# A two-layer network behind attention: the second layer's products, buffers and addresses rearranged

## The chip, the core and the metric

The kernel runs on one core of a Trainium2 chip. That core has a matrix engine (PE; its weight loads are shown apart as PEld), a vector engine (DVE), a scalar engine (ACT), a third elementwise engine (POOL) and a queue engine (SP) that issues most of the transfers; sixteen DMA engines carry those. Matrix products land in PSUM, eight banks of 512 fp32 columns; everything else lies in SBUF, 128 partitions wide. The metric is the device time of one execution in microseconds (us); less is better. A comparison of this kernel can tell about 0.3% from no change.

## The reference

Eight batches of eight heads, 576 tokens, head width 64: causal attention with a decay that is cumulated along the sequence, then a two-layer network with a leaky ReLU whose slope `alpha` differs for each hidden unit.

```python
scores = scale * np.matmul(q, k.transpose(0, 1, 3, 2))
cum = np.cumsum(np.log(np.clip(f, 0.0001, 1.0)), axis=-1)
decay = cum[:, :, :, None] - cum[:, :, None, :]
scores = np.where(causal, -1e9, scores + decay)
attn = softmax(scores)            # row maximum taken off first
x = np.matmul(attn, v)            # -> 4608 tokens x 512
h = x @ w_in                      # 512 -> 2048 hidden units
g = np.maximum(h, 0.0) + alpha * np.minimum(h, 0.0)
out = g @ w_out                   # 2048 -> 512
```

## The kernel before

**Precision.** Most products are made of fp32 numbers cut into a high and a low part in the format fp32r. A product of two such numbers takes three matmuls: high by high, high by low, low by high.

**Attention and the first layer.** For each of 32 pairs of heads the scores, the exponentials and the values are computed; `quotient` writes a normalised x slot. Six x slots of two parts lie in the tile `xx`. `ffn1(b)` takes one batch's 512 tokens through the first layer: 16 blocks `fc` of hidden units, for each 12 matmuls of 512 columns into one bank, then ACT (L1032 or L1035) and for most batches DVE (L1037) move the bank into one of three `hs` slots, and SP writes the slot to the DRAM tensor `hd` (L1039), 2 KB for each partition. The ninth "batch" is the last 64 tokens of each of the eight, gathered in `xt`. The matmuls of `ffn1` are spread between those of the attention from 70 us on, and stand alone from about 545 to 642 us.

**The second layer, `ffn2(u)`.** 18 units `u` of 256 tokens follow each other in the order of `UNITS`. Each is a product of 256 tokens x 2048 by 2048 x 512, cut once into quarters in Winograd's form of Strassen's scheme, so that seven products of 128 tokens by 256 columns stand in place of eight. The 16 blocks of hidden units are paired to eight `c`, taken two at a time: four groups `g`. For each group

- SP loads 512 KB from `hd` into an `hr` slot (L1252), in pieces of 1 KB,
- for the batches in `LATE`, which are 6 of the 18 units, ACT (L1262) and DVE (L1267) finish the leaky ReLU,
- DVE makes the sums S1 to S4 in a `gx` slot (L1272 to L1275, four instructions of 256 columns),
- ACT makes the high parts of the seven operands (L1288, three instructions) in a `gh` slot, and DVE the low parts (L1291, three instructions of 256, 512 and 1024 columns),
- PE runs 2 x 7 products of three matmuls of 256 columns each (L364, from L1306): 42 matmuls.

The weights lie in `wot`, seven combinations for each `c`, with all high parts ahead of all low parts. There are three `gh` slots; the third begins its life when `xx` is free of x. A unit holds four of the eight banks from its first matmul until its end, when ACT copies one half bank (L1314) and DVE adds the banks up in four instructions (L1318, L1319, L1322, L1323) into the single `hs` result, which SP writes out (L1354). The last unit has an end of its own (L1325 to L1345).

**What sets the order.** The class `Plan` holds all operations with estimated times, dependencies and keys, and plays them against each other; the order in which it picks them is the order in which each engine's instructions are issued. Buffers (`Buf`, `Ring`, `Store`) are handed out in that play, banks too. An engine issues its instructions strictly in that order and waits at each for its inputs.

**Addresses.** Five tables of 64 bytes stand ahead of `wi`, so that `wi` and every large tile behind it begin 64 bytes past a multiple of 128.

Of the kernel before, what the change touches and what calls it, by code (L numbers as in the profile page):

```python
# [9 lines left out]
F32 = mybir.dt.float32  # L10
# [195 lines left out]
def attention_moe(  # L206
# [23 lines left out]
    hd = dram.tile([NW, 2, 128, NT], F32, name="hd")  # L230
# [8 lines left out]
    am = const.tile([128, NF], F32, name="am")  # L239
    psum = ctx.enter_context(tc.tile_pool(name="psum", bufs=1, space=PSUM))  # L240
# [4 lines left out]
    xx = xp.tile([128, 6 * 2 * 512], F32R, name="xx")  # L245
# [41 lines left out]
    xs = xp.tile([128, 2 * S], F32, name="xs")  # L287
    rxs = Ring(Store([xs[:, S * i : S * i + S] for i in range(2)]))
    rri = ring(xp, 1, [128, 4, 6, 32], F32, "ri")
# [6 lines left out]
    tri = sp.tile([128, 128], BF16, name="tri")  # L296
    tri2 = sp.tile([128, 64], BF16, name="tri2")
# [717 lines left out]
    def ffn1(b):  # L1015

        for fc in range(NF):
# [16 lines left out]
            else:  # L1034
# [5 lines left out]
                hd[fc % NW, fc // NW, :, 512 * b : 512 * b + 512], bs.t), -1000, [cp], [bs], kb=256)  # L1040
# [79 lines left out]
    rhr = ring_later(2, [128, GW, 2, TU], F32, "hr")  # L1120
    rgx = ring_later(1, [128, 4, GW, 128], F32, "gx")
# [6 lines left out]
    wot = [None] * (NW - NV) + [wid[:, WN * i : WN * i + WN].rearrange("p (k j n) -> p k j n", k=2, j=7) for i in range(NV)]  # L1128

    def change():  # L1130
# [8 lines left out]
        for i in range(NW - NV):  # L1139
            wot[i] = p1.tile([128, 2, 7, 256], F32R, name=f"wot{i}")  # L1140
        rP.least = 0

    def change3():
        st = rhr.store
        for i in range(4):
            st.free.append((plan.t, len(st.items)))
            st.items.append(wx[0].rearrange("p a (b c j) n -> p (a b) c j n", b=2, c=GW)[:, i])

    def change2():
        n = 2 * 7 * GW * 128  # L1150
# [10 lines left out]
    def change5():  # L1161
        rgx.store.free.append((plan.t, len(rgx.store.items)))
        rgx.store.items.append(xs[:, 0:1024].rearrange("p (i c q) -> p i c q", i=4, c=GW))

    o_change = op("-", 0, change, 0, done_a)
    for c in (0, 2):
        bt_ = Buf(rhr)
        tv = lambda bt_=bt_: bt_.t.rearrange("p c j t -> p c (j t)")
        ld = op("SP", 400, lambda c=c, tv=tv: sy.dma_start(tv(), xt[c : c + 2].rearrange("c p t -> p c t")), 1e6, [o_change] + xt_ops, [bt_], kb=512)
        for i in range(2):  # L1170
            bx = Buf(rx)
            xh = op("ACT", c_acs(512), lambda i=i, bx=bx, tv=tv: ac.activation(bx.t[:, 0], tv()[:, i], AF.Copy), 1e4, [ld], [bt_, bx])
            xl = op("DVE", c_dve(512), lambda i=i, bx=bx, tv=tv: ve.tensor_tensor(
                bx.t[:, 1], tv()[:, i], bx.t[:, 0].bitcast(F32), ALU.subtract), 1e4, [xh], [bt_, bx], two=True)
            x_ops[B, c + i] = (bx, xh, xl)
# [9 lines left out]
    def load_w_out(c):  # L1185
# [214 lines left out]
```

## Time and profile before

| | us |
|---|---|
| median of the runs (lowest to highest) | 1012.02 (1010.92 to 1013.88) |
| profiled execution, its own time | 1010.48 |
| profiled execution, span from first to last instruction | 1008.7 |
| busy in the span: PE, PEld | 999.0, 888.5 |
| busy in the span: DVE, ACT, POOL | 803.7, 606.8, 394.6 |

The span falls into three stretches. Up to about 545 us the attention and the first layer are mixed; until 642 us the first layer stands alone; from 642 us to the end there is only the second layer. In that last stretch POOL has nothing to do. The clock granted to PE was full in all of them. Busy times of PE count a matmul until its modelled end, so that overlapping matmuls make a busy engine; rates are better read from the starts or from counts in a stretch.

### The profile page before, as it was taken

The page shows a single profiled execution, that of the slowest core. Times are in us where ns is not written, and L with a number is a line of the kernel's source. Part 1 is how long each engine was busy: PE and PEld are TensorE (multiplying, and loading weights), DVE is VectorE, ACT ScalarE, POOL GpSimd, SP SyncE. Part 2 cuts the span into 40 slices and gives each one's busy share as a digit, 9 for nine tenths or more (in the row PEclk, how much of TensorE's full clock was granted, in tenths as well). Part 3 has the DMA queues.
Part 4 walks back from the last instruction along what each step waited for, and adds up shares of the span by engine and source line. Part 5 has one row for each costly group of instructions (what it writes and reads, how often), then busy time and mean ns, then how long its engine had stood idle before and what let it go on. Part 6 is the DMA issues. An engine that isn't in the chain of part 4 may idle for free.

```text
span 1008.7 us, 22200 instructions
## 1 busy us (share of the span) xinstructions
PE 999.0 (99%) x7900; PEld 888.5 (88%) x7900; DVE 803.7 (80%) x1745; ACT 606.8 (60%) x1369; POOL 394.6 (39%) x635
## 2 busy tenths in 40 slices
PE   9999999999999999999999999999999999999998
PEld 6778888888888788888888888999999999999998
DVE  7878768888877848868655987788898888989994
ACT  7987876666666645656444766564554645546551
POOL 4575758799988858869740100000000000000000
PEclk9999999999999999999999999999999999999999
DMA  7988748889887887968766666633534344434411
GB/s 225 264 241 245 227 130 230 238 250 264 257 242 211 260 242 206 260 206 233 235 174 241 212 205 212 207 116 123 157 113 142 115 140 132 139 115 137 135 55 42
DMA packets 130686, 191.12 MB, mean 189 GB/s; under 512 B 22088, under 2 KB 79728, under 8 KB 130576
## 3 DMA queue, kind: packets, MB, share of 16 engines
q1 hardware_dynamic: 124400, 170.66, 55.7%
q0 software_dynamic: 5888, 18.85, 7.4%
q8 instruction: 62, 1.02, 0.4%
q14 instruction: 48, 0.39, 0.1%
q10 hardware_dynamic: 288, 0.20, 0.1%
HBM read 102.74 MB, written 48.80 MB: 150 GB/s over the span
## 4 chain that ended last, share of the span: by engine, by line
PE 93%; DMA 3%; DVE 2%; ACT 1%; SPq 1%; POOL 1%; issue 0%; DVEq 0%; ACTq 0%
PE bank L364 89%; PE bank L584 2%; DMA big<-big 1%; SPq L920 1%; DVE big L883 1%; DMA rd<-st 0%; DMA vr<-in_vv_dram 0%; PE bank L432 0%; DMA rqk<-in_qk_dram 0%; ACT big L826 0%; DVE Z L491 0%; PE bank L466 0%; POOL Z L510 0%; ACT big L580 0%; POOL Qhl L538 0%
## 5 line engine op out<-in xcount | busy, mean ns | idle before, releaser
L364 PE MATMUL bank<-xx,wi 128*128 128x512 f32 x1728 | 407.7, 392 | 1.8 <-DVE st L846 1.8
L364 PEld LDWEIGHTS bank<-xx,wi 128*128 128x128 f32 x1728 | 319.8, 188 | 68.4 <-DVE st L846 2.2
L826 ACT ACTIVATE big<-big,st 128x384 f32<-128x384 f32 (+4 forms) x207 | 118.6, 575 | 44.3 <-DVE st L846 44.3
L1037 DVE SCALAR_TENSOR_TENSOR hs<-bank,sa,hs 128x512 f32<-128x512 f32 x96 | 71.2, 743 | 79.0 <-ACT hs L1035 78.8
L364 PE MATMUL bank<-wi,gh 128*128 128x256 f32 x1008 | 123.9, 283 | 0.0
L364 PE MATMUL bank<-wot,gh 128*128 128x256 f32 x1008 | 123.9, 283 | 0.0
L364 PEld LDWEIGHTS bank<-wot,gh 128*128 128x128 f32 x1008 | 122.3, 192 | 0.1
L364 PEld LDWEIGHTS bank<-wi,gh 128*128 128x128 f32 x1008 | 122.3, 192 | 0.0
L1035 ACT ACTIVATE hs<-bank,ab 128x512 f32<-128x512 f32 x96 | 66.1, 689 | 88.3 <-PE bank L364 70.5
L883 DVE STREAM_TRANSPOSE big<-big 128x1408 f32<-128x1408 f32 (+2 forms) x69 | 86.6, 1273 | 22.3 <-DMA hd<-hs 6.7
L364 PEld LDWEIGHTS bank<-big,vr 128*64 128x64 f32 x1884 | 88.9, 137 | 12.0 <-issue 3.9
L364 PE MATMUL bank<-big,vr 128*64 128x128 f32 (+2 forms) x1884 | 95.5, 259 | 2.0 <-DVE st L609 1.1
L538 POOL TENSOR_TENSOR Qhl<-rqk,Qhl 128x640 fp32r<-128x640 f32 (+1 forms) x56 | 83.3, 1496 | 30.8 <-ACT Qhl L537 29.1
L920 POOL DMA_DIRECT2D big<-big x184 | 92.1, 507 | 7.9 <-DVE big L883 4.2
L364 PE MATMUL bank<-Qhl 64*128 64x512 f32 (+6 forms) x840 | 93.1, 326 | 0.1
L364 PEld LDWEIGHTS bank<-Qhl 64*128 64x128 f32 (+1 forms) x840 | 74.9, 186 | 15.8 <-issue 9.1
L510 POOL TENSOR_TENSOR Z<-Z,tri 128x384 f32<-128x384 f32 x60 | 54.6, 922 | 27.9 <-DMA Z<-c 18.5
L364 PE MATMUL bank<-wot,xx 128*128 128x256 f32 x504 | 62.4, 283 | 0.0
L364 PE MATMUL bank<-wi,xx 128*128 128x256 f32 x504 | 62.4, 283 | 0.0
L364 PEld LDWEIGHTS bank<-wi,xx 128*128 128x128 f32 x504 | 61.3, 192 | 0.0
L364 PEld LDWEIGHTS bank<-wot,xx 128*128 128x128 f32 x504 | 61.3, 192 | 0.0
L1032 ACT ACTIVATE hs<-bank,sg 128x512 f32<-128x512 f32 x48 | 33.0, 687 | 33.3 <-PE bank L364 28.4
(176 smaller groups left out, 1501.5 us busy)
## 6 DMA issues: line engine op xcount, KB each, us to landing
hd<-hs SPq DMA_DIRECT2D x144, 256.0 KB, 3.6
wx<-hd SPq DMA_DIRECT2D x46, 512.0 KB, 3.8
big<-big SPq DMA_DIRECT2D x184, 100.0 KB, 5.1
big<-big POOLq DMA_DIRECT2D x184, 100.0 KB, 4.9
rqk<-in_qk_dram SPq DMA_DIRECT2D x28, 608.0 KB, 5.1
hr<-hd SPq DMA_DIRECT2D x26, 512.0 KB, 3.5
vr<-in_vv_dram SPq DMA_DIRECT2D x32, 320.0 KB, 4.4
big<-in_w_in_dram SPq DMA_DIRECT2D x16, 512.0 KB, 6.1
```

The source lines that it names most:

```text
L364: pe.matmul(o, lhsT, rhs, start=start, stop=stop)
L510: m1 = op("POOL", c_po(128 * 3), lambda z4=z4: po.tensor_tensor(z4()[:, 6:9], z4()[:, 0:3], tb(3), ALU.add), kc + 0.1, got + [o_mask], [bZ])
L538: o2 = op("POOL", c_po(w), lambda hi=hi, lo=lo, raw=raw: po.tensor_tensor(lo(), raw(), hi().bitcast(F32), ALU.subtract), kc, [o1], [bqk, bQ])
L584: pe.transpose(t[:, c : c + 128], src[:, 128 * j : 128 * j + 128], ident)
L826: sums.append(op("ACT", c_exp(w), lambda: ac.activation(at(), at(), AF.Exp, bias=lo()[:, col : col + 1], scale=-1.0, accum_out=su()[:, col ...
L883: ve.transpose(t_t[:, :, c0 : c0 + 32 * (b1 - b0)].rearrange("p k (b c) -> p k b c", c=32), bE.t[:, 128 * off : 128 * (off + b1 - b0)].rea ...
L920: moves.append(op(n_, 550 if i % 2 else 450, lambda a=a, k=k, q_=q_: q_.dma_start(bM.t[32 * k : 32 * k + 32, a], t_t[32 * a : 32 * a + 32, ...
L1032: cp = op("ACT", c_act(512), lambda bh=bh, bs=bs, fc=fc: ac.activation(bs.t, bh.t, AF.Copy, scale=sg[:, fc : fc + 1]), -1000, [last, o_sg] ...
L1035: cp = op("ACT", c_act(512), lambda bh=bh, bs=bs, fc=fc: ac.activation(bs.t, bh.t, AF.Relu, scale=ab[:, fc : fc + 1]), -1000, [last, o_sg] ...
L1037: cp = op("DVE", c_dve(512), lambda bh=bh, bs=bs, fc=fc: ve.scalar_tensor_tensor(bs.t, bh.t, sa[:, fc : fc + 1], bs.t, ALU.mult, ALU.add), ...
```

## The change

The second layer is rewritten, and tiles change places.

- **Products.** In all units but the last, three of the seven products (numbers 0, 2 and 5) put the high operand against the high and the low weights in one matmul of 512 columns, and then the low operand against the high weights in one of 256. `wot` is laid out so that a combination's high and low parts are neighbours. Such a product fills a whole bank, whose halves are added at the end; a unit holds five banks, taken one after the other as they are first used, and its products run one after the other for both `c` of a group. `rO` may hold all eight banks.
- **The unit's end.** DVE adds one half bank (L1357), the two halves of two banks (L1327, four instructions of 256 columns), then as before (L1330, L1333, L1334): eight instructions in place of four.
- **A group.** Raw and summed operands share a slot of `hg` (8 KB, five slots in the end, in place of six `hr` and two `gx`). The sums take three instructions (512, 256, 256 columns), the high parts two, the low parts one of 1792 columns. The third `gh` slot and one `hg` slot are laid over the old x slots by a pool of their own (`change2`).
- **`hd`** is laid out by batch and group, so that a group's load is two runs of 2 KB for each partition; the first layer's write becomes four runs of 512 bytes.
- **Addresses.** `xx` goes to the upper end of SBUF; `hs`, `xs`, `ri`, `tri` and `tri2` become parts of one tile `hx`; 64 bytes are left free behind the five tables. `wi`, `hx`, `xx`, `big`, `gh`, `hg`, `wx` and `wot` all begin at a multiple of 128 bytes.

The diff, cut to what matters:

```diff
-    hd = dram.tile([NW, 2, 128, NT], F32, name="hd")
+    hd = dram.tile([B + 1, NW // GW, 128, 2, 2, 2, GW, 128], F32, name="hd")
...
+    const.tile([128, NF], F32, name="rest_c")
...
-    xx = xp.tile([128, 6 * 2 * 512], F32R, name="xx")
+    ctx_x = ExitStack()
+    xq = ctx_x.enter_context(tc.tile_pool(name="xq", bufs=1, side="right"))
+    xx = xq.tile([128, 6 * 2 * 512], F32R, name="xx")
+    xq.tile([128, 24], F32, name="rest_x")
...
-    rH, rO = Ring(banks, 2, 4), Ring(banks, 0, 6)
+    rH, rO = Ring(banks, 2, 4), Ring(banks, 0, 8)
...
-    hs = xp.tile([128, 7 * 256], F32, name="hs")
+    hx = xp.tile([128, 3840], F32, name="hx")
+    hs = hx[:, 2048:3840]
...
             hd_ops[b, fc] = op("SP", 400, lambda bs=bs, fc=fc: sy.dma_start(
-                hd[fc % NW, fc // NW, :, 512 * b : 512 * b + 512], bs.t), -1000, [cp], [bs], kb=256)
+                hd[b, fc % NW // GW, :, fc // NW, :, :, fc % GW].rearrange("p u i q -> p (u i) q"), bs.t.rearrange("p (k q) -> p k q", q=128)), -1000, [cp], [bs], kb=256)
...
-            wot[i] = p1.tile([128, 2, 7, 256], F32R, name=f"wot{i}")
+            wot[i] = p1.tile([128, 7, 2, 256], F32R, name=f"wot{i}")
...
-    PRODS = ((0, 0, 3, 0), (1, 1, 2, 0), (2, 6, 0, 1), (3, 3, 1, 0), (4, 5, 1, 1), (5, 4, 2, 1), (6, 2, 0, 0))
+    PRODS = ((0, 0, 3, 0), (2, 1, 2, 0), (1, 6, 0, 1), (4, 3, 1, 0), (3, 5, 1, 1), (5, 4, 2, 1), (6, 2, 0, 0))
...
+        twice = (0, 2, 5) if wide else ()
+        parts = [[PRODS[i] for i in k] for k in ((0,), (1, 5), (3, 4), (2, 6))] if wide else (PRODS[:3], PRODS[3:])
...
-            o2 = op("DVE", 4 * c_dve(128 * GW), sums, key, [o1], [bhr, bgx], two=True)
...
+            h0 = op("ACT", c_acs(3 * 128 * GW), lambda bhx=bhx, bgh=bgh: ac.activation(bgh.t[:, 0, 0:3], bhx.t[:, 1:4], AF.Copy), key, o1, [bhx, bgh])
+            o2 = op("DVE", c_tt(256 * GW) + 2 * c_tt(128 * GW), sums, key, o1, [bhx], two=True)
+            h1 = op("ACT", c_acs(4 * 128 * GW), lambda bhx=bhx, bgh=bgh: ac.activation(bgh.t[:, 0, 3:7], bhx.t[:, 4:8], AF.Copy), key, [o2], [bhx, bgh])
...
+                        if ia in twice:
+                            bank = 4 if ia == 5 else bank
+                            mm(bo[bank].t, bgh.t[:, 0, ia, cc], wot[c][:, ib].rearrange("p k n -> p (k n)"), c == 0, False)
+                            mm(bo[bank].t[:, 0:256], bgh.t[:, 1, ia, cc], wot[c][:, ib, 0], False, c == NW - 1)
+                            continue
...
-        e1 = op("DVE", 2 * c_dve(512), ends, -500, [e0], bo[:3] + [bs])
-        e2 = op("DVE", c_dve(512) + c_dve(256), ends2, -500, [e1], bo[:2] + [bs])
+        e1 = op("DVE", c_tt(256), lambda: ve.tensor_tensor(bs.t[:, 3], bo[3].t[:, :256], bs.t[:, 3], ALU.add), -500, [e0], [bo[3], bs])
+        for i, k in ((0, 2), (4, 4)):
+            e1 = op("DVE", 2 * c_tt(256), lambda i=i, k=k: both(i, k), -500, [e1, ends_of[-5]], [bo[k], bs])
+        e1 = op("DVE", c_tt(512), ends, -500, [e1, ends_of[-3]], [bo[1], bs])
+        e2 = op("DVE", c_tt(512) + c_tt(256), ends2, -500, [e1, last], [bo[0], bo[1], bs])
```

Two places of the order. On PE, one `c` of a group in the second layer before (number 0 in the first unit; `x3` and `x6` count equal matmuls that follow each other, each with its weight load):

```order
L364 MATMUL bank6_82<-wot0_6096,gh0_6093 128x256 x3
L364 MATMUL bank1_77<-wot0_6096,gh0_6093 128x256 x3
L364 MATMUL bank5_81<-wot0_6096,gh0_6093 128x256 x3
L364 MATMUL bank3_79<-wot0_6096,gh0_6093 128x256 x6
```

(the second and the third row follow once more behind these) and after, the first group of the second unit, whose two `c` are `wot0` and `wot1`:

```order
L372 MATMUL bank0_77<-wot0_6095,gh1_6093 128x512
L372 MATMUL bank0_77<-wot0_6095,gh1_6093 128x256
L372 MATMUL bank0_77<-wot1_6096,gh1_6093 128x512
L372 MATMUL bank0_77<-wot1_6096,gh1_6093 128x256
L372 MATMUL bank7_84<-wot0_6095,gh1_6093 128x512
L372 MATMUL bank7_84<-wot0_6095,gh1_6093 128x256
L372 MATMUL bank4_81<-wot0_6095,gh1_6093 128x512
L372 MATMUL bank4_81<-wot0_6095,gh1_6093 128x256
```

Three matmuls of 256 columns became one of 512 and one of 256; behind these rows come the same four for `wot1` and then 24 matmuls of 256 columns into two more banks.

On DVE, the end of a unit among the next groups' work before (L1318 to L1323 are the end):

```order
L1291 TENSOR_TENSOR gh1_6094<-xs_107,gh1_6094 128x1024
L1318 TENSOR_TENSOR hs_92<-bank4_80,hs_92 128x2x256
L1319 TENSOR_TENSOR hs_92<-bank0_76,hs_92 128x512
L1322 TENSOR_TENSOR hs_92<-bank2_78,hs_92 128x512
L1323 TENSOR_TENSOR hs_92<-bank0_76,hs_92 128x256
L1291 TENSOR_TENSOR xx_88<-hr0_6090,xx_88 128x256
```

and after (L1357 to L1334 are the end, with a group's low parts, L1294, in the middle of it):

```order
L1357 TENSOR_TENSOR hx_97<-bank7_84,hx_97 128x256
L1327 TENSOR_TENSOR hx_97<-bank3_80,hx_97 128x256 x2
L1327 TENSOR_TENSOR hx_97<-bank4_81,hx_97 128x256 x2
L1330 TENSOR_TENSOR hx_97<-bank5_82,hx_97 128x512
L1294 TENSOR_TENSOR gh2_6866<-wx_6094,gh2_6866 128x1792
L1333 TENSOR_TENSOR hx_97<-bank1_78,hx_97 128x512
L1334 TENSOR_TENSOR hx_97<-bank5_82,hx_97 128x256
L1294 TENSOR_TENSOR gh0_6092<-wx_6094,gh0_6092 128x1792
```

The end has eight instructions in place of four, and it begins while the unit's last group still runs. Until the last batches of the first layer the order of every engine is the same as before.

## Rows read from the trace of the kernel before

**Rows 1.** Page, part 1: busy us, share of the span, instructions.

```profile
PE 999.0 (99%) x7900; PEld 888.5 (88%) x7900; DVE 803.7 (80%) x1745; ACT 606.8 (60%) x1369; POOL 394.6 (39%) x635
```

**Rows 2.** Stretches: length, busy us (instructions) by engine, granted clock, DMA share, GB/s.

```profile
230.00:340.00 110.00, 107.75 (x916) 89.97 (x914) 86.34 (x212) 68.17 (x183) 95.34 (x156) 1.00 0.85 246
700.00:750.00 50.00, 50.00 (x419) 50.00 (x418) 44.01 (x80) 26.56 (x48) 0.00 (x0) 1.00 0.42 131
```

**Rows 3.** The chain that ended last: 283 to 341 us by line; its piece behind that.

```profile
by line: DMA big<-big 22.0%; SPq L920 13.5%; DVE big L883 10.2%; DMA rd<-st 7.7%; DMA rqk<-in_qk_dram 7.2%; ACT big L826 6.0%; issue 3.9%; DVE Z L491 3.9%; POOL Z L510 3.0%; POOL Qhl L538 2.5%; PE bank L364 2.3%; DVE Zt L493 2.3%; POOL xx L
...
340.57 664.55 PE bank L364 x5064
```

**Rows 4.** A stretch of 10 us in the first layer alone, PE only.

```profile
560.00:570.00 10.00, 10.00 (x46) 1.00 0.83 262
```

**Rows 5.** PE in the second layer, in order of time: start, us, line, tiles, shape, count.

```profile
702.55 10.24 PE L364 MATMUL bank<-wot,gh 128*128 128x256 f32 x84
712.63 5.20 PE L364 MATMUL bank<-wi,xx 128*128 128x256 f32 x42
```

**Rows 6.** Groups by line and shape: busy us, mean ns, idle before.

```profile
L364 PE MATMUL bank<-xx,wi 128*128 128x512 f32 x1728 | 407.7, 392 | 1.8 <-DVE st L846 1.8
L1291 DVE TENSOR_TENSOR gh<-gx,gh 128x1024 fp32r<-128x1024 f32 x24 | 29.3, 1219 | 2.0 <-ACT gh L1288 2.0
L1291 DVE TENSOR_TENSOR gh<-wx,gh 128x256 fp32r<-128x256 f32 x34 | 14.2, 418 | 0.0
L1267 DVE TENSOR_TENSOR wx<-wx,gx 128x1024 f32<-128x1024 f32 x7 | 8.5, 1220 | 0.0
```

**Rows 7.** DVE in order of time: a unit's end, a group's low parts, sums.

```profile
702.45 0.69 DVE L1318 TENSOR_TENSOR hs<-bank,hs 128x512 f32<-128x512 f32 x1 [2.22 <-ACT xx L1288]
703.17 0.69 DVE L1319 TENSOR_TENSOR hs<-bank,hs 128x512 f32<-128x512 f32 x1
703.96 0.69 DVE L1322 TENSOR_TENSOR hs<-bank,hs 128x512 f32<-128x512 f32 x1
704.56 0.41 DVE L1323 TENSOR_TENSOR hs<-bank,hs 128x256 f32<-128x256 f32 x1
704.89 1.02 DVE L1291 TENSOR_TENSOR xx<-hr,xx 128x256 fp32r<-128x256 f32 x2
705.83 1.22 DVE L1291 TENSOR_TENSOR xx<-gx,xx 128x1024 fp32r<-128x1024 f32 x1
706.97 0.42 DVE L1272 TENSOR_TENSOR xs<-hr 128x256 f32<-128x256 f32 x1
707.64 0.42 DVE L1274 TENSOR_TENSOR xs<-xs,hr 128x256 f32<-128x256 f32 x1
708.09 0.43 DVE L1275 TENSOR_TENSOR xs<-hr,xs 128x256 f32<-128x256 f32 x1
708.43 1.02 DVE L1291 TENSOR_TENSOR gh<-hr,gh 128x256 fp32r<-128x256 f32 x2
```

**Rows 8.** DVE busy in three units that follow each other.

```profile
745.80:766.00 20.20, 17.70 (x34) 1.00 0.42 131
766.00:786.10 20.10, 18.07 (x37) 1.00 0.41 131
786.10:806.30 20.20, 18.70 (x32) 1.00 0.42 132
```

**Rows 9.** Who DVE waited for, 645 to 988 us: total us, times, longest.

```profile
DVE hs L1318 <- ACT xx L1288: 10.6, 5, 2.2
DVE gh L1291 <- ACT gh L1288: 6.2, 7, 1.2
```

**Rows 10.** Queue q1 in 627:640, 713:718.5 and 1006.2:1008.2 us: packets, MB, share of 16 engines.

```profile
q1 hardware_dynamic: 774, 1.47, 29.8%
q1 hardware_dynamic: 528, 0.52, 31.9%
q1 hardware_dynamic: 288, 0.20, 31.8%
```

More of the change, by code (lines that the diff above doesn't have):

```diff
@@ L1127, in attention_moe @@
     WN = 7 * 2 * 256
[L1128 removed]
+    wot = [None] * (NW - NV) + [wid[:, WN * i : WN * i + WN].rearrange("p (j k n) -> p j k n", k=2, j=7) for i in range(NV)]
     def change():
@@ L1161, in change5 @@
     def change5():
-        rgx.store.free.append((plan.t, len(rgx.store.items)))
-        rgx.store.items.append(xs[:, 0:1024].rearrange("p (i c q) -> p i c q", i=4, c=GW))
+        more(hx[:, 0:2048])
     o_change = op("-", 0, change, 0, done_a)
[L1166 to L1175, printed above, removed]
+    bt_ = Buf(rhx)
+    tv = lambda: bt_.t.rearrange("p (c e) g q -> p c (e g q)", c=4)
+    ld = [op("SP", 400, lambda c=c: sy.dma_start(tv()[:, c : c + 2], xt[c : c + 2].rearrange("c p t -> p c t")), 1e6, [o_change] + xt_ops, [bt_], kb=512) for c in (0, 2)]
+    for c in range(NC4):
+        bx = Buf(rx)
+        xh = op("ACT", c_acs(512), lambda c=c, bx=bx: ac.activation(bx.t[:, 0], tv()[:, c], AF.Copy), 1e4, [ld[c // 2]], [bt_, bx])
+        xl = op("DVE", c_dve(512), lambda c=c, bx=bx: ve.tensor_tensor(
+            bx.t[:, 1], tv()[:, c], bx.t[:, 0].bitcast(F32), ALU.subtract), 1e4, [xh], [bt_, bx], two=True)
+        x_ops[B, c] = (bx, xh, xl)
     for b in range(B + 1):
@@ L1293, in ffn2 @@
             seen = set()
-            todo = [(cc, part) for cc in range(GW) for part in (PRODS[:3], PRODS[3:])]
+            todo = [(cc, part) for part in parts for cc in range(GW)] if wide else [(cc, part) for cc in range(GW) for part in parts]
             if u == UNITS[-1] and g == NW // GW - 1:
@@ L1304, in prods @@
                             seen.add(bank)
-                            end = c == NW - 1 and n == 2 and (bank == 3 or (ia, bank) in ((6, 0), (4, 1), (5, 2)))
-                            mm(o, bgh.t[:, ka, ia, cc], wot[c][:, kb, ib], first, end)
-                last = op("PE", 3 * len(part) * c_mm(256), prods, key + m / 20,
-                          [last] + his + rdy + wo_ready[c], bo + [bgh])
+                            end = c == NW - 1 and n == 2 and (bank == 3 or (ia, bank) in ((6, 0), (3, 1), (5, 2)))
+                            mm(o, bgh.t[:, ka, ia, cc], wot[c][:, ib, kb], first, end)
+                last = op("PE", 3 * len(part) * c_mm(256) - 13 * sum(x[0] in twice for x in part), prods, key + m / 20,
+                          [last] + his + rdy + wo_ready[c], [bo[k] for k in bo if k in {4 if wide and x[0] == 5 else x[2] for x in part}] + [bgh])
                 ends_of.append(last)
```

109 lines of the change are left out of this document (53 added, 56 removed).

## The prediction

> **What bounds the kernel now.** I read the page's busy times first: PE is busy for 999.0 of 1008.7 us, and no other engine for more than 80% [rows 1]. An average over stages hides which engine is close behind, so I read single stretches next. In the second layer PE is busy for all of 50 us and DVE for 44.0 of them [rows 2]; over three units that follow each other DVE is busy for 17.70, 18.07 and 18.70 of some 20.2 us [rows 8]. The chain of waits says the same from the other side: from 340.57 us on, 664.55 us of it are one run of PE matmuls, and only between 283 and 341 us does it run through transfers, POOL and DVE [rows 3]. So in the second layer the time is the number of matmuls times the spacing of their starts, as long as DVE, at 90%, keeps up. Both terms are touched by the change.
>
> **The spacing of matmuls.** In the second layer 84 matmuls of 256 columns start at 702.55 us and the next 42 at 712.63 [rows 5]: 10.08 us / 84 = 120.0 ns each, and a group of 42 takes 5.04 us, a unit of four groups 20.16 us. In the first layer alone, 46 matmuls of 512 columns fit in 10 us [rows 4]: 217.4 ns each. Two matmuls of 256 columns cost 240.0 ns, one of 512 costs 217.4: a matmul that is twice as long hides its successor's weight load better. One merged product saves 22.6 ns.
>
> **Part 1, the merged matmuls.** 17 units x 8 `c` x 3 products = 408 merged pairs; 408 x 22.6 ns = 9.2 us. A group then takes 24 x 120.0 + 6 x (217.4 + 120.0) = 4904 ns, a unit 19.62 us. The trace has no stream that alternates 512 and 256 columns, so I bound it. Least: the mean busy time of a 512 matmul over the whole kernel is 407.7 / 1728 = 235.9 ns [rows 6], which would leave 4.1 ns, or 1.7 us in all. Most: the 256-column matmul behind a 512 pays no wait for its weights, and costs half of 217.4 ns; the saving is 360 - 326.1 = 33.9 ns, or 13.8 us. I take 9.2, since the rate of the pure 512 stream has the same engine doing the same thing, while 235.9 mixes in the attention.
>
> **Part 2, DVE's work.** I count from start to start, which is what a busy engine pays. Before: a group's low parts take 0.94 us for the first two (704.89 to 705.83) and 1.14 for the third, the four sums 1.46 (706.97 to 708.43), 3.54 in all; the unit's end takes 2.44 (702.45 to 704.89) [rows 7]. A unit is 4 x 3.54 + 2.44 = 16.6 us, and one of the six late units has four more of 1.22 [rows 6].
> After, from the same rows: an instruction of 512 columns takes 0.60 from start to start (703.96 to 704.56), one of 256 about 0.34 (two starts lie between 706.97 and 707.64), and one that needs the result of the one before it about 0.12 more (707.64 to 708.09 is 0.45). The sums become 0.60 + 0.12 + 0.34 + 0.12 + 0.34 = 1.52. The low parts as one of 1792: from 418 ns at 256 and 1219 ns at 1024 [rows 6] each column costs 1.04 ns, so 1.14 + 768 x 1.04 ns = 1.94. A group takes 3.46, 0.08 less. The end is five instructions of 256 with four dependent ones (5 x 0.34 + 4 x 0.12 = 2.18), and then the old last three (703.17 to 704.89, 1.72): 3.90, 1.46 more. Sum: 17.7 us, 1.1 more than before. Added to the measured mean of rows 8 (18.16): 19.3 of 19.6 us. DVE has some 0.3 us to spare for each unit where it had 2.0.
>
> **Does PE then wait for DVE?** Two things could make it. Operands: three `gh` slots let DVE run one to two groups ahead. When PE frees a slot, ACT needs about 2 us for two high parts and DVE 1.94 for the low part; PE comes back to it after two groups, 9.8 us. Some 5 to 6 us are left for whatever stands ahead in DVE's order. A late unit takes 4 x 1.22 = 4.9 us more, of which 1.9 are covered (19.6 - 17.7); it sets DVE back by 3.0, and the two units behind it win back 3.8. Banks: four and four made eight, so a new unit never waited; five and five make ten. The fourth bank of a new unit is needed 6 x 337 ns = 2.0 us after its start, the fifth after 3.5; they come free with the first and third instruction of the old unit's end, which can start some 4 and 3 us before it. That leaves about 5 us again. I expect PE to stay fed but for a little near the close, where two late units lie two apart: 0.5 us, between 0 and 5.
>
> A rule that speaks against this: by the Trainium skill, "VectorE: DVE Perf Modes", section "The DRAIN you can't avoid", the next DVE instruction does not start until the pipe of the one before is empty. The trace shows starts 0.34 us apart for instructions of 0.42 [rows 7], so here they overlap. If instructions paid their whole length, DVE would need about 19.7 us for a unit, 0.1 more than PE, and the sum would end 1.5 us later, at 1005.7.
>
> **Part 3, the first layer's writes.** A write to `hd` becomes 512 packets of 512 bytes in place of 128 of 2 KB; a load 256 of 2 KB in place of 512 of 1 KB. From the queue's shares [rows 10]: 0.298 x 16 x 13 us = 62.0 us for 1.47 MB of mostly 2 KB packets, 86 ns for each; 0.319 x 16 x 5.5 = 28.1 us for 512 of 1 KB, 54 ns; and 10.2 us for 128 of 1 KB and 128 of 512 bytes, which leaves at most 26 ns for the small ones. A line through 86 and 54 would give 38. A write then holds each DMA engine for 512 x 26 / 16 = 0.83 to 1.22 us where it was 0.69. 144 writes x 0.14 to 0.53 us are 20 to 76 us, 4 to 13% of the 572 us over which they are spread. Mostly that is hidden, since PE has other work; it shows where the chain runs through transfers, from 283 to 341 us. There DMA pieces are 22.0 + 7.7 + 7.2 = 37% of 58 us, 21 us [rows 3], and the DMA share is 0.85 [rows 2]. 4 to 13% of 21 us is 0.9 to 2.8; nothing, if they queue behind other things. I take 0.9, by the row of packets of the same size. The loads become cheaper by 0.35 us of each DMA engine, in a stretch with a share of 0.42 [rows 2]: nothing.
>
> **Edits that I cost at nothing.** ACT's two high parts for three, in a stretch where ACT is busy for 26.6 of 50 us [rows 2]. DVE's repeated wait for an earlier write of the same `hs` slot, which ACT has already waited for. The sums of `w_out`: as many, as long. SP's queue: five `hg` slots for six `hr`, still five groups of lead for loads that take about 4 us. The last unit and the end of the kernel: unchanged. Addresses: every large tile lay at the same offset before, so no row can compare two; DVE's and PE's rates above are for that offset. I take nothing, and bound it below.
>
> **Sum.** -9.2 + 0.5 + 0.9 = -7.8 us. The profiled execution (span 1008.7, 1010.48 in all, 1.8 around the span) would become 1002.7; it lies 1.5 under the median of 1012.02, which gives **1004.2**.
>
> **Rivals.**
> - *DVE takes over, slower.* Between 645 and 988 us DVE is idle for about 35 us, mostly in waits that stand at fixed places of its order: 10.6 us at a unit's end behind ACT, 6.2 at low parts behind ACT, and smaller ones [rows 9]. If these stem from the order, and not from DVE being ahead, they stay: 18.16 + 1.1 + 1.8 = 21.1 us for a unit, 0.9 more than before: 17 x 0.9 + 0.9 = 16, up to 1028. It is slower from the point at which more than 0.9 us of idle time remain for each unit. For it: the new end waits for PE at three places. Against: DVE waits there because it is ahead, and a DVE that is behind finds its inputs ready. 0.14.
> - *Addresses help.* If the 256-column pair's 120.0 ns holds a cost of the offset, it could fall to 108.7 at best; PE's unit to 18.3 us, and DVE would hold it at 19.3: 17 x 0.3 + 168 x 11 ns = 7 us more, 997, or less if the attention gains as well. No row speaks for it. 0.09.
> - *The merged matmul brings little.* At 235.9 ns the sum is -1.7 + 1.4: 1011.7. Against: the pure stream. 0.07.
> - *Small packets, or new neighbours among addresses, cost 3 to 10 us* in the attention, where POOL, DVE and DMA are closest: 1007 to 1014. 0.15.
> - *As forecast*, 1001 to 1007: 0.55.
>
> About 0.3% (3 us) is what can be told from no change. Faster by more, under 1009.0: 0.55 + 0.09 + about half of 0.15 = 0.71; within it: 0.07 + the other half = 0.15; slower: 0.14. The range leaves out most of the first rival and some of the second: 995 to 1012.
>
> **What would show it.** A right step 1: a group of the second layer takes 4.90 us from start to start, PE is still busy throughout, and the stretch from the end of the first layer to the last matmul is 9 us shorter. A right step 2: DVE busy for about 19.3 of 19.6 us, and no wait of PE for DVE or for a bank at a unit's start. A right step 3: the last matmul of the first layer ends within 1 us of 642. Wrong if PE shows idle time at unit starts (first rival), if 256-column matmuls start at another spacing than 120.0 ns, or if the first layer ends early or late by more than 3 us.

## The result, and the profile after

The changed kernel takes 1017.21 us (median; 1016.23 to 1018.97) against 1010.96 of the kernel before on the same chip: 1.0056 times as long, interval 1.0042 to 1.0071. The prediction said 1004.2 and faster; the time lies outside its range. The profiled execution has a span of 1014.7 us, 6.0 more than before.

PE is still the bound. Part 1 of the page after (busy us, share, instructions) answers [rows 1]:

```profile
PE 1004.0 (99%) x7492; PEld 866.9 (85%) x7492; DVE 815.2 (80%) x1597; ACT 593.0 (58%) x1297; POOL 394.5 (39%) x635
```

408 matmuls fewer, and 5.0 us more busy. Where they went is read from PE in order of time. First the kernel before (start, us, what, count), the end of the first layer and the start of the second:

```profile
535.87 106.38 PE L364 MATMUL bank<-xx,wi 128*128 128x512 f32 x468
642.08 10.23 PE L364 MATMUL bank<-wot,gh 128*128 128x256 f32 x84
```

Then the changed kernel, the same place and four double groups of the second layer (a row of `x72` is a double group: two groups of 36 matmuls each), which answer [rows 5]:

```profile
542.95 109.46 PE L372 MATMUL bank<-xx,wi 128*128 128x512 f32 x468
652.25 10.00 PE L372 MATMUL bank<-wot,gh 128*128 128x512 f32 x71
...
692.10 10.11 PE L372 MATMUL bank<-wot,gh 128*128 128x512 f32 x72
702.05 10.11 PE L372 MATMUL bank<-wi,gh 128*128 128x512 f32 x72
712.00 10.16 PE L372 MATMUL bank<-wot,gh 128*128 128x512 f32 x72
722.00 10.11 PE L372 MATMUL bank<-wi,gh 128*128 128x512 f32 x72
```

The second layer starts at 652.25 instead of 642.08, 10.2 us late. It is 4.05 us shorter: before, the last group starts at 999.91 and takes 5.04 (end 1004.95, 362.87 in all); after, the last two start at 1001.05 and take 10.02 (end 1011.07, 358.82 in all). 10.2 - 4.05 is the 6 us of the span, to within 0.1.

Little of the 10.2 us is lost in a wait: over the whole span PE is idle for 10.7 us where it was for 9.7. The same 468 matmuls of 512 columns, one behind the other, take 652.25 - 542.95 = 109.30 us where they took 106.21: 233.5 ns each, and 226.9 before. (The expectations below write 233.3 and 226.7.) No matmul of this stretch was changed. The other 1260 of the first layer, between pieces of the attention, are slower too: where one follows the other, the median spacing is 232 ns instead of 227. So the delay grows all along. Stretches of the changed kernel (length, busy us (instructions) of PE, PEld, DVE, ACT, POOL, granted clock, DMA share, GB/s) answer [rows 2, 4]:

```profile
230.00:340.00 110.00, 106.03 (x897) 88.06 (x897) 84.61 (x210) 66.40 (x180) 92.98 (x152) 1.00 0.89 243
560.00:570.00 10.00, 10.00 (x45) 8.03 (x44) 9.82 (x14) 6.12 (x10) 3.58 (x2) 1.00 0.38 111
700.00:750.00 50.00, 50.00 (x364) 47.26 (x363) 47.66 (x66) 26.77 (x40) 0.00 (x0) 1.00 0.42 135
```

The granted clock is 1.00 of the upper level (2.4 GHz) in all of them, so the clock is not the reason. In the second line PE shows 45 matmuls where [rows 4] show 46. That view counts every matmul that touches the stretch, at its modelled length of nearly 0.4 us: (10.0 + 0.39) us / 226.9 ns is 45.8. The prediction read 10 us / 46 = 217.4 ns from it, which never was a spacing. (The section on the time before says that rates can be read from counts in a stretch; for a stretch as short as this one they can't.)

The chain that ended last (start, us, what), against [rows 3]:

```profile
231.31 3.39 DMA hd<-hx
...
246.15 6.62 DMA hd<-hx
...
264.36 11.37 DMA rqk<-in_qk_dram
...
282.52 9.44 DMA rqk<-in_qk_dram
...
319.53 691.71 PE bank L372 x4840
```

It runs through transfers from 231 us on, where the chain before had one transfer at 228 us and then none until 283, and it leaves them at 319.5 instead of 340.6. Most of the delay comes behind them: PE instructions of the same number in both traces start 1.7 us later at 228 us, 4.1 at 348 and 10.2 at 642.

DVE did what was foreseen, and PE shows no wait in the second layer. DVE's instructions in one group of the changed kernel, and three stretches of a unit's length, against [rows 7, 8]:

```profile
701.41 0.69 DVE L1283 TENSOR_TENSOR hg<-hg 128x512 f32<-128x512 f32 x1
702.13 0.42 DVE L1284 TENSOR_TENSOR hg<-hg 128x256 f32<-128x256 f32 x1
702.59 0.43 DVE L1285 TENSOR_TENSOR hg<-hg 128x256 f32<-128x256 f32 x1
702.93 2.02 DVE L1294 TENSOR_TENSOR gh<-hg,gh 128x1792 fp32r<-128x1792 f32 x1
704.87 2.02 DVE L1294 TENSOR_TENSOR gh<-hx,gh 128x1792 fp32r<-128x1792 f32 x1
```

```profile
745.80:765.70 19.90, 19.25 (x26) 1.00 0.41 129
765.70:785.60 19.90, 18.48 (x28) 1.00 0.39 136
785.60:805.50 19.90, 18.59 (x25) 1.00 0.41 133
```

### The profile page after: what moved, and what is told of

It is laid out like the page before. It is cut to its first block, busy times and chain, and to the rows that moved or that the text cites. A ratio compares the mean times of both kernels' runs of the same rounds, so it can differ in the third digit from the quotient of the medians.

```text
span 1014.7 us, 21097 instructions
## 1 busy us (share of the span) xinstructions
PE 1004.0 (99%) x7492; PEld 866.9 (85%) x7492; DVE 815.2 (80%) x1597; ACT 593.0 (58%) x1297; POOL 394.5 (39%) x635
## 4 chain that ended last, share of the span: by engine, by line
PE 91%; DMA 5%; DVE 2%; SPq 1%; issue 1%; POOL 1%; ACT 1%; DVEq 0%; POOLq 0%
PE bank L372 87%; DMA rqk<-in_qk_dram 3%; PE bank L592 2%; DMA hd<-hx 1%; DMA hx<-rd 1%; SPq L928 1%; PE bank L440 0%; DVE big L891 0%; DMA vr<-in_vv_dram 0%; DMA big<-big 0%; POOL hx L990 0%; DVE Z L499 0%; PE bank L474 0%; POOL xx L997 0%; DVE big L854 0%
## 5 line engine op out<-in xcount | busy, mean ns | idle before, releaser
L372 PE MATMUL bank<-wi,gh 128*128 128x256 f32 (+1 forms) x1308 | 182.3, 300 | 0.0
L372 PE MATMUL bank<-wot,gh 128*128 128x256 f32 (+1 forms) x1308 | 182.3, 300 | 0.0
L372 PEld LDWEIGHTS bank<-wot,gh 128*128 128x128 f32 x1308 | 171.4, 190 | 9.4
L372 PEld LDWEIGHTS bank<-wi,gh 128*128 128x128 f32 x1308 | 171.4, 190 | 9.3
L1045 DVE SCALAR_TENSOR_TENSOR hx<-bank,sa,hx 128x512 f32<-128x512 f32 x96 | 71.3, 745 | 85.4 <-ACT hx L1043 85.2
L1043 ACT ACTIVATE hx<-bank,ab 128x512 f32<-128x512 f32 x96 | 65.8, 688 | 96.2 <-PE bank L372 72.5
L518 POOL TENSOR_TENSOR Z<-Z,hx 128x384 f32<-128x384 f32 x60 | 54.7, 925 | 29.6 <-DMA Z<-c 18.1
L1294 DVE TENSOR_TENSOR gh<-hg,gh 128x1792 fp32r<-128x1792 f32 x28 | 56.5, 2017 | 1.6 <-ACT gh L1293 1.6
L1294 DVE TENSOR_TENSOR gh<-wx,gh 128x1792 fp32r<-128x1792 f32 x28 | 56.2, 2018 | 0.0
L997 POOL TENSOR_TENSOR xx<-hx,xx 128x512 fp32r<-128x512 f32 x32 | 42.0, 1322 | 30.5 <-ACT xx L996 30.1
```

Source lines behind the costliest of these rows:

```text
L372: pe.matmul(o, lhsT, rhs, start=start, stop=stop)
L518: m1 = op("POOL", c_po(128 * 3), lambda z4=z4: po.tensor_tensor(z4()[:, 6:9], z4()[:, 0:3], tb(3), ALU.add), kc + 0.1, got + [o_mask], [bZ])
L997: xl = op("POOL", c_po(512), lambda: po.tensor_tensor(bx.t[:, 1], bxs.t[:, 0:512], bx.t[:, 0].bitcast(F32), ALU.subtract), st, [xh], [bxs, ...
L1043: cp = op("ACT", c_act(512), lambda bh=bh, bs=bs, fc=fc: ac.activation(bs.t, bh.t, AF.Relu, scale=ab[:, fc : fc + 1]), -1000, [last, o_sg] ...
L1045: cp = op("DVE", c_dve(512), lambda bh=bh, bs=bs, fc=fc: ve.scalar_tensor_tensor(bs.t, bh.t, sa[:, fc : fc + 1], bs.t, ALU.mult, ALU.add), ...
L1294: his, rdy = [h0, h1], [op("DVE", c_tt(7 * 128 * GW), lambda bhx=bhx, bgh=bgh: ve.tensor_tensor(bgh.t[:, 1], bhx.t[:, 1:8], bgh.t[:, 0].bi ...
```

## Experiments: what slows the 512-column matmuls

The theories at the start: **A**, the start addresses (large tiles at a multiple of 128 bytes) make the matmuls slower; **B**, the place of `xx` at SBUF's end does; **C**, the 512-byte packets of `hd` or the rest of the change do. In every run the 468 matmuls before the second layer show the spacing free of waits.

**e1** is the kernel before, with everything above the tables 64 bytes lower:

```diff
-    am = const.tile([128, NF], F32, name="am")
+    rest = ctx.enter_context(tc.tile_pool(name="rest", bufs=1, side="right"))
+    am = rest.tile([128, NF], F32, name="am")
```

> The kernel before with one 64-byte table moved to SBUF's end, so that everything above it begins 64 bytes lower: wi, xx, hs and the later tiles then stand at a multiple of 128 bytes instead of 64 bytes past one. Nothing else is changed. Theory A (start addresses): the first layer's 512-column matmuls, which start every 226.7 ns in the trace of before and every 233.3 ns in that of the changed kernel, go to about 233 ns here too; 1728 of them x 5.5 to 6.6 ns = 9.5 to 11.4 us, so the second layer starts near 652 us instead of 642.1 and the time is about 1021 us. Theory B (place of xx at the far end) and theory C (the 512-byte packets and other parts of the change): 226.7 ns stays, 1011 us.

**e2** and **e3**, the changed kernel with one of the two operands 64 bytes off, and **e4** with both:

```diff
-    const.tile([128, NF], F32, name="rest_c")            # e2, e4
...
-    xq.tile([128, 24], F32, name="rest_x")
+    xq.tile([128, 8], F32, name="rest_x")                # e3, e4
...
-        p2.tile([128, 24], F32, name="rest_p")
+        p2.tile([128, 8], F32, name="rest_p")            # e4
```

> The changed kernel without its 64 bytes of padding below: wi, hx and everything between them and the end stand 64 bytes past a multiple of 128 again, xx at the far end stays at a multiple of 128. If the address of the weights wi (loaded as the stationary operand) decides: 226.7 ns between 512-column matmuls, second layer from about 643 us, time about 1006 us. If the address of xx (streamed as the moving operand), or its place at the far end, decides, or the packets do: 233 ns and about 1017 us.

> The changed kernel with 64 bytes less behind xx, so that xx alone begins 64 bytes past a multiple of 128, wi and the others at a multiple. If the address of the moving operand xx decides: 226.7 ns, first layer 10 us shorter, second layer as in the changed kernel, about 1007 us. If that of wi, the far end, or the packets: 233 ns and about 1017 us.

> The changed kernel with both: no padding below, and all tiles at the far end 64 bytes further, so that every large tile begins 64 bytes past a multiple of 128, as in the kernel before. Theory A: 226.7 ns in the first layer, second layer from 642 to 643.5 us, and in the second layer 226.7 + 120.0 = 346.7 ns for a merged pair against 360 ns of three separate matmuls, 408 x 13.3 ns = 5.4 us less than before; the time 1005 to 1007 us. Theories B and C: about 1017 us, as the changed kernel.

PE at the end of the first layer (start, us, what, count) in e1, e2, e3 and e4:

```profile
536.68 106.38 PE L365 MATMUL bank<-xx,wi 128*128 128x512 f32 x468
642.89 10.24 PE L365 MATMUL bank<-wot,gh 128*128 128x256 f32 x84
```

```profile
545.10 109.46 PE L371 MATMUL bank<-xx,wi 128*128 128x512 f32 x468
654.40 7.83 PE L371 MATMUL bank<-wot,gh 128*128 128x512 f32 x53
```

```profile
542.49 109.47 PE L372 MATMUL bank<-xx,wi 128*128 128x512 f32 x468
651.80 10.11 PE L372 MATMUL bank<-wot,gh 128*128 128x512 f32 x72
```

```profile
541.50 106.38 PE L371 MATMUL bank<-xx,wi 128*128 128x512 f32 x468
647.71 10.15 PE L371 MATMUL bank<-wot,gh 128*128 128x512 f32 x72
```

e1 keeps 226.9 ns with all tiles at a multiple of 128: 1010.04 us, ratio to the kernel before 0.998 (0.9969 to 0.9991). So A falls. e2 (1016.63, 1.0045, 1.003 to 1.006) and e3 (1016.39, 1.005, 1.003 to 1.007) keep 233.5: neither operand's own address decides. e4 is back at 226.9 with `xx` still at SBUF's end and the packets still small: 1010.46 us, 0.9994 (0.9978 to 1.001). B falls, and C for this term. What orders the runs is the *distance* from `wi` to `xx`: 65536 bytes in the kernel before and in e1, 203264 in e4, both multiples of 512; 203136 in the changed kernel (128 past a multiple of 256), 203200 in e2 and e3 (192 past). That is theory **D**. (The second layer of e4 starts at 647.71 for another reason: by the starts of equal PE instructions, its profiled execution lost 5.8 us between 288 and 300 us, was 5.6 us behind the kernel before at 348 us, and lost nothing more until the second layer. Its median is 2.9 us below that execution's time.)

**e6** and **e5** test D in the kernel before, where `wi` alone is moved:

```diff
-    ab = const.tile([128, NF], F32, name="ab")
-    am = const.tile([128, NF], F32, name="am")
...
     wi = xp.tile([128, NF, 2, NC4, 128], F32R, name="wi")
+    ab = xp.tile([128, NF], F32, name="ab")
+    am = xp.tile([128, NF], F32, name="am")
     xx = xp.tile([128, 6 * 2 * 512], F32R, name="xx")
```

(e6; e5 moves `sg` and `sa` as well.)

> The kernel before with wi alone 128 bytes lower: two 64-byte tables that stood below wi now stand between wi and xx; xx and all that follows keep their addresses, the distance from wi to xx is 65664 bytes (128 more than a multiple of 512) instead of 65536. Theory D (the distance of the two operands decides, not where each begins): the first layer's 512-column matmuls go from 226.7 to about 233 ns, the second layer starts near 652 us, the time is about 1020 to 1022 us. Theory B (the place of xx at the far end, away from wi) or C: 226.7 ns, 1011 us.

> The same with four tables moved, so that wi is 256 bytes lower and the distance is 65792 bytes, a multiple of 256 but not of 512. Of theory D, which of the two is the period: if 256 bytes, 226.7 ns and 1011 us; if 512, about 233 ns and 1020 to 1022 us.

e6, then e5, PE in order of time:

```profile
542.53 109.45 PE L364 MATMUL bank<-xx,wi 128*128 128x512 f32 x468
651.82 10.23 PE L364 MATMUL bank<-wot,gh 128*128 128x256 f32 x84
```

```profile
536.36 106.38 PE L364 MATMUL bank<-xx,wi 128*128 128x512 f32 x468
642.57 10.24 PE L364 MATMUL bank<-wot,gh 128*128 128x256 f32 x84
```

With 128 bytes more between the two, and nothing else, the spacing is 233.5 ns and the second layer starts at 651.82, 9.7 us later than before: 1016.33 us, 1.0054 (1.0038 to 1.007). With 256 more it is 226.9 and 1011.46 us, 1.0006 (0.9993 to 1.002). So D holds, with a period of 256 bytes. The time of e6 was missed: 1020 to 1022 foreseen, 1016.3 found. Its second layer became 2.0 us shorter as well, which was the next question; and its profiled execution, from which the 9.7 us are read, is the slowest of its four (1018.15 us). By the medians the first layer lost 5.35 + 2.0 = 7.4 us.

How much of the 10.2 us is the distance? From 348 us to the second layer PE runs the same instructions in all runs, 1028 of the 1728 matmuls of 512 columns among them. Over this stretch the changed kernel falls 6.03 us further behind the kernel before, e6 5.92, e2 and e3 6.59; every run at distance 0 (by which a multiple of 256 is meant) keeps its lag to within 0.01 us. These 6 us are the distance. Of the 4.15 us that the changed kernel has lost by 348 us its part can't be told: the runs at distance 0 lag there too, e1 and e5 by 0.8 and 0.5, those with the code of the changed kernel by 1.2 to 5.6.

## Experiments: the second layer

e6 gave the first sign. In its second layer half of the weights lie in `wi`, which had moved, and half in `wot`, which had not:

```profile
722.03 5.15 PE L364 MATMUL bank<-wi,xx 128*128 128x256 f32 x42
727.01 5.15 PE L364 MATMUL bank<-wi,gh 128*128 128x256 f32 x42
732.00 5.20 PE L364 MATMUL bank<-wot,gh 128*128 128x256 f32 x42
737.03 5.20 PE L364 MATMUL bank<-wot,xx 128*128 128x256 f32 x42
```

The groups with `wi`, at distance 128, take 4.98 and 4.99 us (118.7 ns a matmul); those with `wot`, at distance 0, 5.03 and 5.04.

In e4 every distance of `gh` to the weights is a multiple of 256, and a double group takes 10.00 us; in the changed kernel two of three take 9.95. There `gh2` stands 128 past a multiple of 256 from the weights, and the double groups with `gh2` in them are the short ones. **e9** and **e10** shift all `gh` slots; they also have **e8**'s layout of `hd`, which is told below:

```diff
+            if name == "gh":
+                p1.tile([128, 48], F32, name="rest_g")   # e10: 16
             r.store.items += [p1.tile(shape, dt, name=f"{name}{i}") for i in range(n)]
+            if name == "gh":
+                p1.tile([128, 16], F32, name="rest_h")   # e10: 48
...
-        p2.tile([128, 8], F32, name="rest_p")
+        p2.tile([128, 24], F32, name="rest_p")           # e10: 56
```

> The kernel of e8 (2 KB runs, wi to xx a multiple of 512 bytes apart) with the second layer's gh slots moved by 64 bytes against the weights wot: 192 instead of 0 bytes past a multiple of 256 from them. In the changed kernel the groups whose gh slot stands 128 bytes off took 4.952 us against 5.000 on it, in e2 those 192 bytes off 4.930 us. Theory D2 (the distance acts on the second layer's matmuls too, there the other way): all 68 groups 4.92 to 4.94 us, 4.1 to 5.4 us less than e8, time 1003.5 to 1004.5 us; the first layer stays at 226.7 ns. Rival (those groups were short because the slot stands at the far end, or because groups with another distance stood beside them): 5.00 us in two of three groups, 1007 us.

> As e9, with gh 64 instead of 192 bytes past a multiple of 256 from wot. If only the fact counts that the distance is no multiple of 256: groups of 4.93 to 4.95 us, time 1003.5 to 1005 us. If the sign of the distance counts: 5.00 us or more, 1008.7 us or later.

Double groups of e4 (`gh` 0 bytes past a multiple of 256 from the weights), e9 (192) and e10 (64), PE in order of time:

```profile
697.70 10.16 PE L371 MATMUL bank<-wi,gh 128*128 128x512 f32 x72
707.70 10.16 PE L371 MATMUL bank<-wot,gh 128*128 128x512 f32 x72
```

```profile
693.42 10.00 PE L371 MATMUL bank<-wi,gh 128*128 128x512 f32 x72
703.26 10.00 PE L371 MATMUL bank<-wot,gh 128*128 128x512 f32 x72
```

```profile
692.72 10.06 PE L371 MATMUL bank<-wi,gh 128*128 128x512 f32 x72
702.61 10.06 PE L371 MATMUL bank<-wot,gh 128*128 128x512 f32 x72
```

A group takes 5.00, 4.92 and 4.947 us, whichever slot it reads. e9: 1004.20 us, 0.9914 (0.9888 to 0.994); e10: 1004.81, 0.9924 (0.99 to 0.9947). The own address of `gh` doesn't decide: `gh0` and `gh1` begin at the same byte in the changed kernel and in e10, where the weights lie elsewhere, and their groups take 5.00 and 4.947 us. The distance acts here too, the other way round: of the distances measured, the best for the stream of 512 columns is the worst for this one.

The labels of e9 and e10 count from the weights to `gh`. Here `gh` is what PE loads (PEld's 128x128) and the weights are streamed, while in the first layer `wi` is loaded and `xx` streamed. Counted as there, from the loaded to the streamed operand, e9's distance is 64 and e10's 192.

**e12** takes e9's merged matmuls apart again, so that the distance stays and the merge goes:

```diff
-    mm(bo[bank].t, bgh.t[:, 0, ia, cc], wot[c][:, ib].rearrange("p k n -> p (k n)"), c == 0, False)
+    mm(bo[bank].t[:, 0:256], bgh.t[:, 0, ia, cc], wot[c][:, ib, 0], c == 0, False)
+    mm(bo[bank].t[:, 256:512], bgh.t[:, 0, ia, cc], wot[c][:, ib, 1], False, False)
```

> The kernel of e9 with each merged pair of the second layer taken apart again: three matmuls of 256 columns instead of one of 512 and one of 256, all else the same. What is the merge itself worth, at this distance of the operands? If 256-column matmuls keep 117.8 ns: the group 42 x 117.8 ns = 4.947 us against 4.920 us merged, 68 groups 1.8 us more, 1006.0 us. If the merge saves the 13.3 ns a pair that the spacings of the kernel before say (226.7 + 120.0 against 3 x 120.0): 5.4 us more, 1009.6 us.

**e14** is e9 once more, on the chip of e12 and e13.

> The kernel of e9 again, beside e12 and e13 on one chip: 1004.2 us, group 4.920 us, 512-column matmuls of the first layer at 226.7 ns.

```profile
694.86 10.06 PE L371 MATMUL bank<-wi,gh 128*128 128x256 f32 x84
704.75 10.06 PE L371 MATMUL bank<-wot,gh 128*128 128x256 f32 x84
```

Here 84 matmuls of 256 columns take 9.89 us, 117.8 ns each; at distance 0 they took 120.0 [rows 5]. e12 comes to 1006.21 us (0.9926, 0.9905 to 0.9947), e14 to 1003.34 (0.9907, 0.9886 to 0.9928). By the traces the merge is worth 4.947 - 4.920 = 27 ns a group, 1.8 us in all; by the medians 2.9 us, with intervals that overlap.

**e7** and **e11** ask why a 512-column matmul costs more among 256-column ones: in e4 236.6 ns on the mean from its start to the next, and 226.9 in the first layer. They reorder the merged products of a group of e4 (`two_` lists the three of a `c`):

```diff
-        parts = [[PRODS[i] for i in k] for k in ((0,), (1, 5), (3, 4), (2, 6))] if wide else (PRODS[:3], PRODS[3:])
+        parts = [[PRODS[i] for i in k] for k in ((0, 1, 5), (3, 4), (2, 6))] if wide else (PRODS[:3], PRODS[3:])
...
+                    for ia, ib, o in two_:                                    # e7
+                        mm(o, bgh.t[:, 0, ia, cc], wot[c][:, ib].rearrange("p k n -> p (k n)"), c == 0, False)
+                    for ia, ib, o in two_:
+                        mm(o[:, 0:256], bgh.t[:, 1, ia, cc], wot[c][:, ib, 0], False, c == NW - 1)
...
+                    for ia, ib, o in two_:                                    # e11, once a group
+                        for d in range(GW):
+                            mm(o, bgh.t[:, 0, ia, d], wot[c + d][:, ib].rearrange("p k n -> p (k n)"), c + d == 0, False)
+                        for d in range(GW):
+                            mm(o[:, 0:256], bgh.t[:, 1, ia, d], wot[c + d][:, ib, 0], False, c + d == NW - 1)
```

> The changed kernel with all large tiles 64 bytes past a multiple of 128 (distance wi to xx 203264 bytes, a multiple of 512), and with the second layer's six merged pairs of a group in another order: three 512-column matmuls one after another, then their three 256-column ones, instead of 512, 256, 512, 256. If a 512-column matmul costs 236.6 ns there because of its 256-column neighbour (226.7 ns among its own kind): two of three pairs come to about 346.7 ns, the group gets 4 x 8 = 32 ns shorter, 68 groups 2.2 us, the time about 1008 us. If the 236.6 ns come from the accumulation or from the operands' places, nothing changes: about 1010.5 us.

> The kernel of e7 with the merged products of both chunks of a group together: 512, 512, 256, 256 of one product into one bank, then the next product. In the first layer twelve 512-column matmuls in a row go to one bank, at 226.7 ns each. If 234 to 241 ns of a 512-column matmul in the second layer come from the change of bank behind it: the first of each two takes 226.7 ns, the group 4.96 us or less, about 1008 us. If from a change between 512 and 256 columns: about 4.98 us as in e7, 1009.4 us. If neither, 5.00 us and 1010.5 us.

Two double groups of e7; then two of e11, the second with a wait:

```profile
693.49 10.12 PE L371 MATMUL bank<-wi,gh 128*128 128x512 f32 x72
703.45 10.12 PE L371 MATMUL bank<-wot,gh 128*128 128x512 f32 x72
```

```profile
683.74 10.08 PE L371 MATMUL bank<-wot,gh 128*128 128x512 f32 x72
693.66 0.63 PE L371 MATMUL bank<-wi,gh 128*128 128x512 f32 x2
694.45 9.75 PE L371 MATMUL bank<-wi,gh 128*128 128x256 f32 x70 [0.16 <-DVE gh L1293]
```

The group is 4.98 us in e7 (1009.44 us, 0.998, 0.9968 to 0.9991) and 4.96 in e11. So order counts at distance 0, by 20 and 40 ns of 5.00 us. Among a group's twelve matmuls of merged products the width changes 11, 3 and 5 times in e4, e7 and e11, the bank 4, 11 and 2 times; neither count alone puts the three in their order. What makes a 512-column matmul dearer there stays open. What e11's shorter groups win is lost again: in the third group of each of the six late units, where DVE has more to do, PE waits for DVE's low parts behind its first two matmuls (the third line shows one such wait). The second layer takes 362.9 us, and the time is 1013.29 (1.0011, 0.9997 to 1.0026).

**e8** against e4, and **e13** against e14, price the 512-byte packets. e8 gives `hd` its old layout and reads it in two transfers a group; e13 is the changed kernel with nothing but e4's and e9's addresses.

```diff
-    hd = dram.tile([B + 1, NW // GW, 128, 2, 2, 2, GW, 128], F32, name="hd")
+    hd = dram.tile([NW, 2, 128, NT], F32, name="hd")
...
-                hd[b, fc % NW // GW, :, fc // NW, :, :, fc % GW].rearrange("p u i q -> p (u i) q"), bs.t.rearrange("p (k q) -> p k q", q=128)), -1000, [cp], [bs], kb=256)
+                hd[fc % NW, fc // NW, :, 512 * b : 512 * b + 512], bs.t), -1000, [cp], [bs], kb=256)
...
```

> The changed kernel with all large tiles 64 bytes past a multiple of 128, and hd in the layout of before: the hidden tiles are written in runs of 2 KB (36864 packets fewer) and read in runs of 1 KB, in two transfers a group. If the 512-byte packets cost what the prediction said (0.9 us in the stretch from 283 to 341 us): about 1009.5 us against 1010.5 with them. If they cost 3 us or more (rival): 1007.5 us or less. If nothing: 1010.5 us.

> The changed kernel with its 512-byte runs of hd kept and only addresses changed: wi to xx a multiple of 512 apart, gh 192 bytes past a multiple of 256 from wot. Against e14 in the same call it prices the 512-byte packets: as predicted, 0.9 us, 1005.1 us; nothing, 1004.2 us; the rival's 3 us or more, 1007.2 us or later.

e8: 1008.70 us (0.9978, 0.9965 to 0.9991), 1.8 under e4, which was measured on another chip; the intervals of the two ratios overlap. e13: 1004.04 us (0.9915, 0.9893 to 0.9936), 0.7 over e14 on the same chip. Both fit the 0.9 us of the prediction, and both fit nothing. The traces say the same: at 348 us, behind the stretch where the packets could cost, the runs with small packets at distance 0 lag the kernel before by 5.6, 1.6, 2.0 and 1.2 us (e4, e7, e11, e13), those with 2 KB by 1.9, 2.1, 1.2, 3.3 and 1.4 (e8, e9, e10, e12, e14). So the packets are not what costs; but all nine lag by over 1 us, so something else in the change may cost 1 to 2 us in the attention. No run tells what. The end of e13's first layer, for comparison with the changed kernel's above:

```profile
537.06 106.37 PE L371 MATMUL bank<-xx,wi 128*128 128x512 f32 x468
643.27 10.00 PE L371 MATMUL bank<-wot,gh 128*128 128x512 f32 x72
```

The same code as the changed kernel, with some paddings of other sizes, is thus 8.9 us faster than the kernel before on the same chip, and 13 us faster than the changed kernel, by medians that were not taken side by side.

## Why the prediction was wrong, step by step

- **The bound** was right: PE, by the number of matmuls times their spacing.
- **The spacing of 512 columns** was mis-sized. 217.4 ns came from a count that includes matmuls across both edges of the stretch; from starts it is 226.9. With that alone the saving of a pair is 360 - (226.9 + 120.0) = 13.1 ns instead of 22.6, 5.3 us instead of 9.2. Starts were used for the 256-column matmuls, in the same paragraph, and gave their 120.0 ns correctly.
- **Part 1** then gave 4.05 us: the mean group takes (722.00 - 652.25) / 14 = 4.982 us, 58 ns under 5.04, where 4.904 was foreseen. At equal distance (e4) it is only 40 ns, 6.7 a pair, so 2.7 us in all; the rest is `gh2`'s new distance. The bounds of the prediction (4.1 and 33.9 ns a pair) do enclose 6.7. Its argument for the upper half, that the pure stream does the same thing, failed: among 256-column matmuls one of 512 takes 236.6 ns (e4).
- **Part 2, DVE,** was right. The sums and the low part take 1.52 and 1.94 us from start to start (701.41 to 702.93, and on to 704.87), foreseen 1.52 and 1.94; DVE is busy 18.5 to 19.3 us of a unit of 19.9, foreseen 19.3 of 19.6; PE waits for nothing in the second layer, foreseen 0.5 us. The first rival did not come. On the rule of the Trainium skill, "VectorE: DVE Perf Modes", "The DRAIN you can't avoid": starts lie 0.34 us apart behind an instruction of 0.43 (702.59 to 702.93), so here too they overlap. The section itself goes on, "A next op that is not held starts earlier", which the prediction left out; with that the trace agrees.
- **Part 3, the packets,** foreseen at 0.9, is 0 to 2 us by e8 and e13, and shows no cost in the traces: not the cause.
- **Addresses** are the step that failed: "every large tile lay at the same offset before, so no row can compare two ... I take nothing". It looked at where each tile begins. What counts is how far the two operands of a matmul lie apart, and moving `xx` to the far end changed that from 65536 to 203136 bytes. Nothing was taken for 1728 matmuls, of which the last 1028 became 6.03 us / 1028 = 5.9 ns longer on the mean, and 6.6 where they stand alone. Of the rivals, "new neighbours among addresses, cost 3 to 10 us" (0.15) has the size about right, but another place and another mechanism: the cost lies in the first layer's PE stream, not in the attention's transfers. "Addresses help" (0.09) was right in its premise, that 120.0 ns hold a cost of the addresses; moving `gh` by 64 bytes gives 2.2 ns of it back (e12). In the change two of three slots stayed at distance 0.
- **What would show it** worked: "if the first layer ends early or late by more than 3 us" points at the right place.

The sum by its own steps, corrected from the traces: +6.0 (the distance in the first layer, from 348 us on) + 4.2 (ahead of that: the distance again, and what single executions differ by, not told apart) - 2.7 (the merge at distance 0, 40 ns x 68) - 1.3 (`gh2`'s distance) = +6.2; the medians differ by 6.25.

That e13 ends at 1004.0 us does not make 1004.2 right: that is luck. Of its 8.9 us, 2 to 3 come from the merge, where 9.2 were foreseen, and the larger part from the distances, where nothing was.

## What to carry to other kernels

A change of addresses can change PE's time like a change of code: where a stream of matmuls sets the time, work out the distance from its stationary operand (the loaded one) to its moving one (the streamed one) modulo 256 bytes before and after, and try the 64-byte steps; it is a padding of one line. Read a spacing from starts, over a long run of equal instructions without a wait between them, never from a count in a short stretch: the instructions across its edges count as well, 2 of 46 here. And when work is merged, price the merge beside the same work unmerged at the same addresses (e12), or its gain is mixed with what the move did.

## What was not expected of the hardware

PE's spacing depends on the distance of the two operands modulo 256 bytes, by up to 3%, and the best of the values measured is another one for each stream. The distance is counted from the loaded operand to the streamed one, `wi` to `xx` in the first layer and `gh` to the weights in the second:

| distance mod 256 | first layer, 512 columns, one after another | second layer, 256 columns, one after another | group of the merged second layer |
|---|---|---|---|
| 0 | 226.9 ns (before, e1, e4, e5) | 120.0 ns (before) | 5.00 us (e4) |
| 64 | not measured | 117.8 ns (e12) | 4.92 us (e9) |
| 128 | 233.5 ns (after, e6) | 118.7 ns (e6, groups with `wi`) | 4.95 us (after, with `gh2`) |
| 192 | 233.5 ns (e2, e3) | not measured | 4.947 us (e10) |

All are at a granted clock of 1.00, with no wait between the matmuls. That a step of 256 bytes changes nothing was tested in the first layer alone (e5). Whether the streams differ by the width of their matmuls or by something else, and what in the chip makes the distance count, no run here tells; that it is a meeting of the weight load with the running matmul is only a guess. The Trainium skill, "SBUF — State Buffer", section "Operand start alignment", asks that an operand begin at a multiple of its element size and says that this concerns legality, not speed; every tile here fulfils it, and the speeds still differ.
